# Block 0 of the convolution kernels: each group's doubling and products behind its own powers, and three modulation vectors computed in the convolution stage

## The chip, the cores and the metric

One core of one Trainium2 chip. Its engines run beside each other, each through its own instructions in a fixed order, and wait for each other by semaphores: TensorE (matmuls, and the loads of their stationary operand), VectorE, ScalarE (functions from tables, and copies), GpSimd, and the queues that start DMA transfers, of which SyncE's (SP) and GpSimd's are used here. The metric is the device time of one execution in microseconds; less is better. A kernel's time is the median of several runs.

## The reference

A sequence x of 2048 tokens by 576 channels passes two residual branches, each behind a layer norm that a conditioning vector c modulates. The first branch is a diagonal state space model, computed as a long convolution; the second a dense layer of width 4608 with relu:

```
mod = silu(c) @ w_mod                   # 6 vectors of 576: sa, ca, ga, sb, cb, gb
h = layernorm(x) * (1 + ca) + sa
dt = exp(log_dt);  A = -exp(log_A_real) + 1j*A_imag;  C = (C_real + 1j*C_imag) * dt
K[d, l] = 2 * Re( sum_n C[d, n] * exp(A[d, n] * dt[d] * l) )     # n < 128, l < 2048
x = x + ga * ( causal_convolution(h, K) + h * D_skip )           # by FFT in the reference
h = layernorm(x) * (1 + cb) + sb
x = x + gb * ( relu(h @ w1) @ w2 )
```

All of it is in 32-bit floating point.

## The kernel before, in words

The convolution kernels K are built first. Position l is split into a high and a low part, so that exp(A dt l) is a product of a factor W1 (16 high parts, with C in it) and a factor W2 (32 low parts), and K is a small matmul over the 128 states for each channel. The 576 channels go through in six groups of 96 (`first`), and the 2048 positions in four blocks of 512. `first` makes block 0; W1, W2 and the higher powers are also written to memory (`W1d`, `W2d`, `Zd`), from which `rest` builds the other blocks later.

For one group g:

- `turns`: six small pairs of matmuls give the phase in turns for 22 exponents; ScalarE rounds them to integers (k) and VectorE subtracts (L143). The matmuls go to three PSUM banks (tag "ph"), which the products' bank and the modulation's also come from.
- `exps`: ten pairs of matmuls in the same banks, and exp on ScalarE.
- `half_values`, once for the odd and once for the even low parts: sine and cosine on ScalarE, and products with the exponentials, the sines' on VectorE (L177, L178), the cosines' on GpSimd. With the odd half goes `start`, which writes the first column of W1 (L201, L202). There are two W1 buffers.
- `powers`: sines and cosines of four powers into a PSUM tile Z, of which there is one, times the exponentials (L216).
- `doubling`: W1 grows from 1 to 2, 4, 8 and 16 columns by complex products with Z on VectorE (L241 to L245); the adds of the last step are on GpSimd.
- `products`: 384 matmuls, each of 16 columns, in pairs for one channel (L255). `rows` copies the result for storing.

ScalarE's operations in this stage are kept in the order in which the program is written; on the other engines a scheduler sets the order, by its own estimates and by what depends on what, and from then on it is fixed. The scheduler sees the tiles: a tile from a pool of n buffers waits until the tile n places before it is no longer used. In the loop over g the program writes: odd values of g+1, rows of g-1, first half of the doubling of g, even values of g+1, second half of the doubling of g, powers of g+1, turns and exponentials of g+2, products of g.

The modulation vectors come from a generator (`mod`), which the group stage advances: silu(c) is spread over 128 columns (cb) and multiplied with a vector's part of w_mod, two halves of ten matmuls each. It makes ga, ca, sa, sb and cb in the group stage, their weights lying in the five W2 buffers. gb is made by `mod_gb` at the end of block 0's convolution. This convolution (`conv(0)`) loads x, normalizes it, transforms it and the kernel by matmuls and VectorE butterflies, multiplies, transforms back, adds, normalizes again (with cb and sb) and transposes the result for the dense layer. Its tiles lie where those of the group stage lay, so it starts when that stage has ended. Then `ffn` runs the dense layer for four blocks of 512 tokens (first matmul hps, L892, second acc, L917), with `rest` and the convolutions of the later blocks between its matmuls.

Of the kernel before, what the change touches and what calls it, by code (L numbers as in the profile page):

```python
# [10 lines left out]
F32 = mybir.dt.float32  # L11
# [7 lines left out]
P = 128  # L19
L = 2048  # L20
D = 576
# [18 lines left out]
class KGen:  # L40
# [19 lines left out]
    def setup(self, I):  # L60
        nc, pc, k = self.nc, self.pc, self.k
        v = nc.vector.tensor_tensor
        tmp = lambda n: self.pt.tile([G, NG, P], F32, tag="W1", bufs=2, name=n)
        lar, ai = tmp("lar"), tmp("ai")
# [67 lines left out]

    def turns(self, g):

        F = []
        for s0, n in ((0, 8), (17, 8), (32, 6)):
            k = self.pt.tile([P, 8, G], I32, tag="k", bufs=3, name=f"k_{g}")[:, :n]
            f = k.bitcast(F32)
            for a in (0, n // 2):
                b = a + n // 2  # L140
                ph = self.times(g, self.zz[0], s0 + a, n // 2)
                self.act(k[:, a:b], ph, AF.Copy)
                self.nc.vector.tensor_tensor(f[:, a:b], ph, k[:, a:b], op=ALU.subtract)  # L143
            F.append(f)
        return F

# [73 lines left out]
    def doubling(self, g):  # L220
# [4 lines left out]
        for i, m in enumerate((1, 2, 4, 8)):  # L225
# [5 lines left out]
            for u in (slice(0, 1), slice(1, 2)) if m > 2 else (slice(0, 2),):  # L231
# [13 lines left out]
                add(out[:, u, :, 1], t[:, :, :, 1], T[:, :, :, 0], op=ALU.add)  # L245
            if m == 2:
                yield

# [14 lines left out]
    def first(self, mod):  # L263

        nc, k = self.nc, self.k
        self.W1, self.Z, W2s, EF, ke = {}, {}, {}, {}, None

        def raw(g):
            if g < NG:
                F = self.turns(g)  # L270
                EF[g] = self.exps(g), F

        def odd(g):
            if g < NG:
                E, F = EF[g]
                W2s[g] = [
                    self.pt.tile([P, 2, 32, H], F32, tag="W2", bufs=5, name=f"W2_{2 * g + u}")
                    for u in range(2)
                ]
                self.half_values(g, W2s[g], E[2:4], F[0], True)  # L280

        def even(g):
            if g < NG:
                E, F = EF[g]
                self.half_values(g, W2s[g], E[0:2], F[1], False)
                for u in range(2):
                    nc.sync.dma_start(
                        out=k.W2d[2 * g + u], in_=W2s[g][u].rearrange("p r b c -> p (r b c)")
                    )

        def pw(g):
            if g < NG:
                E, F = EF.pop(g)
                self.powers(g, E[4], F[2])
                zs = self.Z[g][1]
                for u in range(2):
                    nc.sync.dma_start(out=k.Zd[2 * g + u], in_=zs[:, :, :, u * H : u * H + H])
# [12 lines left out]
        even(0)  # L310
        pw(0)
        next(mod)
        raw(1)
        ps = None
        for g in range(NG):
            odd(g + 1)
            if ps is not None:
                rows(g - 1, ps)
            step = self.doubling(g)
            next(step)  # L320
            next(mod, None)
            even(g + 1)
            next(step, None)
            for u in range(2):
                nc.sync.dma_start(
                    out=k.W1d[2 * g + u], in_=self.W1[g][:, u].rearrange("p a r c -> p (a r c)")
                )
            pw(g + 1)
            raw(g + 2)
            if g % 3 == 0:  # L330
                ke = self.pt.tile([P, 16, 72], F32, tag="ke", bufs=1, name=f"ke_{g}")
            ps = self.bank(f"kps_{g}")[:, :384].rearrange("p (q a) -> p q a", a=16)
            for u in range(2):
                self.products(ps, self.W1[g], W2s[g][u], u)
        rows(NG - 1, ps)

# [106 lines left out]
class Body:  # L443
# [41 lines left out]
    def mod(self, kg):  # L485
# [9 lines left out]
        for i, nm in names:  # L495
            w = ws[nm] = pt.tile([P, 5, D], F32, tag="W2", bufs=5, name=f"wm_{nm}")
            self.mod_weights(w, slice(i * D, (i + 1) * D))
# [6 lines left out]
        yield  # L504
        m = {}
        ga = kg.pc.tile([P, 2, PC], F32, name="m_ga")
        for i, nm in names:
            t = ga if nm == "ga" else self.cst.tile([P, 2, PC], F32, name=f"m_{nm}")
            for h in range(2):
                ps = kg.bank(f"mps_{nm}")[:, :PC]  # L510
                self.mod_product(ps, cb, ws[nm][:, :, h * PC : (h + 1) * PC])
                if nm == "ca":
# [3 lines left out]
                elif nm == "sa":  # L516
                    nc.vector.tensor_tensor(t[:, h], ps, ga[:, h], op=ALU.mult)
                elif nm == "cb":
                    nc.vector.tensor_scalar(t[:, h], ps, 1.0, None, op0=ALU.add)
                else:  # L520
                    nc.vector.tensor_copy(t[:, h], ps)
            m[nm] = t
            self.m = {k: v.rearrange("p h c -> p (h c)") for k, v in m.items() if k != "ga"}
            yield
# [15 lines left out]

    def mod_gb(self):

        cb = self.half("cb").rearrange("p a b -> p (a b)")[:, : 5 * P]
        cb = cb.rearrange("p (k c) -> p k c", c=P)
        self.mod_lhs(cb)
        t = self.m["gb"]
        for h in range(2):
            w = self.spec("wm_gb").rearrange("p a b c -> p (a b c)")[:, : 5 * PC]
            w = w.rearrange("p (k c) -> p k c", c=PC)
            self.mod_weights(w, slice(5 * D + h * PC, 5 * D + (h + 1) * PC))  # L550
            ps = self.cps.tile([P, 512], F32, tag="cps", name="mps_gb")[:, :PC]
            self.mod_product(ps, cb, w)
            self.nc.scalar.activation(t[:, h * PC : (h + 1) * PC], ps, AF.Copy)

    def main(self, ctx, kg):
        nc, tc = self.nc, self.tc
        self.sm = ctx.enter_context(tc.tile_pool(name="sm", bufs=1))
        self.m["gb"] = self.sm.tile([P, D], F32, name="m_gb")
        self.fcU, self.fcK, self.gc = (
# [535 lines left out]
```

## Time and profile before

| | us |
|---|---|
| median of 3 runs | 1543.28 (1539.92 to 1550.67) |
| the profiled execution | 1545.74, of it the span 1543.9 |
| TensorE matmuls busy in the span | 1311.2 (85%) |
| VectorE | 928.5 (60%) |
| ScalarE | 480.2 (31%) |
| GpSimd | 168.5 (11%) |

The stages in the span: setup and groups from 0 to 229, block 0's convolution to 329.7, then the dense layer. Busy shares over the whole span say little about the first two stages, in which every engine has idle time; the rows below are taken from these stages. A row's line number is that of the kernel before.

### The profile page before, as it was taken

What the parts mean: (1) busy time and instruction counts of PE and PEld (TensorE: products, weight loads), DVE (VectorE), ACT (ScalarE), POOL (GpSimd) and SP (SyncE); (2) the same over time, 40 slices, a digit from 0 to 9 for tenths busy, and PEclk for the clock granted to TensorE, in tenths of its full rate; (3) what the DMA queues carried; (4) which work ended last, traced back from release to release, by engine and by line L of the source; (5) the groups of instructions that cost most, each with busy time, mean ns of one, the idle gap of its engine ahead of it and who ended that gap; (6) DMA issues with size and microseconds to landing.
All of it is one profiled execution on the core that took longest, in us unless ns stands there. A gap on an engine that the chain in (4) does not pass through costs nothing.

```text
span 1543.9 us, 26164 instructions
## 1 busy us (share of the span) xinstructions
PE 1311.2 (85%) x10664; PEld 1036.8 (67%) x10664; DVE 928.5 (60%) x1396; ACT 480.2 (31%) x885; POOL 168.5 (11%) x271
## 2 busy tenths in 40 slices
PE   6665534379998899669899999999999999999997
PEld 4455433257787677447677777777787788888885
DVE  4645457979975558876684688936499831111112
ACT  4645414022222134014222432243432233233221
POOL 1433431000001010000101001000000000000000
PEclk9766656689999999779999999999999999999998
DMA  6533356346769758436986889667699656766662
GB/s 211 214 129 129 145 221 248 134 157 213 264 219 374 254 191 327 168 146 189 351 292 211 286 322 330 230 177 254 212 341 366 221 172 196 213 195 196 198 196 70
DMA packets 116903, 345.99 MB, mean 224 GB/s; under 512 B 19568, under 2 KB 21008, under 8 KB 105776
## 3 DMA queue, kind: packets, MB, share of 16 engines
q1 hardware_dynamic: 98432, 218.88, 43.4%
q0 software_dynamic: 18128, 124.86, 21.5%
q8 instruction: 83, 1.36, 0.4%
q10 hardware_dynamic: 224, 0.59, 0.1%
q14 instruction: 36, 0.29, 0.1%
HBM read 260.53 MB, written 83.76 MB: 223 GB/s over the span
## 4 chain that ended last, share of the span: by engine, by line
PE 51%; DVE 19%; issue 18%; DMA 9%; ACT 2%; POOL 1%; SPq 0%; POOLq 0%; ACTq 0%; DVEq 0%
PE hps L892 18%; PE acc L917 17%; PE kps L399 5%; PE ps_f L628 3%; PE ph L117 3%; DVE Y L759 2%; DVE T L757 2%; DMA w<-L1d 2%; DMA w<-L2d 2%; PE kps L255 2%; PE ps_i L766 1%; DMA Ud<-U 1%; DMA kt<-kd 1%; DVE T L242 1%; DMA L1d<-w 1%
## 5 line engine op out<-in xcount | busy, mean ns | idle before, releaser
L917 PE MATMUL acc<-hh,w 128*128 128x512 f32 x1296 | 429.7, 406 | 7.7 <-DMA w<-L2d 4.9
L892 PE MATMUL hps<-xh,w 128*128 128x512 f32 x1152 | 394.8, 403 | 0.0
L917 PE MATMUL acc<-hl,w 128*128 128x512 f32 x720 | 284.4, 408 | 20.9 <-DVE hl L898 20.8
L898 DVE SCALAR_TENSOR_TENSOR hl<-hps,hh 128x512 fp32r<-128x512 f32 x144 | 98.8, 686 | 323.8 <-ACT hh L897 323.6
L917 PEld LDWEIGHTS acc<-hh,w 128*128 128x128 f32 x1296 | 245.7, 191 | 63.6 <-DMA w<-L2d 6.2
L892 PEld LDWEIGHTS hps<-xh,w 128*128 128x128 f32 x1152 | 219.3, 192 | 47.5
L892 PE MATMUL hps<-xl,w 128*128 128x512 f32 x576 | 232.1, 403 | 0.0
L897 ACT ACTIVATE hh<-hps 128x512 fp32r<-128x512 f32 x144 | 86.1, 598 | 354.6 <-PE hps L892 351.9
L875 ACT ACTIVATE w<-r 128x576 fp32r<-128x576 f32 x144 | 98.8, 686 | 282.4 <-issue 188.0
L917 PEld LDWEIGHTS acc<-hl,w 128*128 128x128 f32 x720 | 137.7, 192 | 51.6 <-DVE hl L898 22.3
L892 PEld LDWEIGHTS hps<-xl,w 128*128 128x128 f32 x576 | 110.5, 192 | 23.7
L866 ACT ACTIVATE w<-r 128x640 fp32r<-128x640 f32 x144 | 105.3, 732 | 31.1 <-DMA L1d<-w 23.5
L892 PE MATMUL hps<-xs,w 128*128 128x512 f32 x288 | 101.3, 420 | 11.6 <-DMA w<-L1d 6.9
L399 PEld LDWEIGHTS kps<-W1r,W2r 128*32 128x32 f32 x3456 | 69.3, 146 | 37.8 <-issue 28.8
L399 PE MATMUL kps<-W1r,W2r 128*32 128x48 f32 (+2 forms) x3456 | 79.9, 238 | 12.6 <-issue 11.7
L759 DVE TENSOR_TENSOR Y<-Y,T 128x1152 f32<-128x1152 f32 x64 | 84.5, 1348 | 0.1
L629 ACT ACTIVATE Z<-ps_f 128x288 f32<-128x288 f32 x128 | 52.1, 409 | 78.7 <-PE ps_f L628 76.4
L117 PE MATMUL ph<-dl,zt 96*128 96x384 f32 (+1 forms) x72 | 22.9, 469 | 61.7 <-DVE k L143 50.8
L892 PEld LDWEIGHTS hps<-xs,w 128*128 128x128 f32 x288 | 54.2, 193 | 26.7 <-DMA w<-L1d 8.6
L766 PE MATMUL ps_i<-V,gc 128*128 128x288 f32 x128 | 43.9, 482 | 32.7 <-DVE V L642 14.8
L255 PE MATMUL kps<-W,W 128*32 128x16 f32 x2304 | 39.3, 216 | 36.1 <-issue 24.8
L628 PE MATMUL ps_f<-kt,fcK 128*128 128x288 f32 x128 | 46.2, 465 | 27.7 <-DVE kt L700 18.0
(177 smaller groups left out, 1515.7 us busy)
## 6 DMA issues: line engine op xcount, KB each, us to landing
r<-in_w_dram SPq DMA_DIRECT2D x144, 320.0 KB, 3.6
r<-in_w_dram SPq DMA_DIRECT2D x144, 288.0 KB, 3.3
w<-L1d SPq DMA_DIRECT2D x108, 320.0 KB, 3.0
w<-L2d SPq DMA_DIRECT2D x108, 288.0 KB, 3.2
W2r<-W2d POOLq DMA_DIRECT2D x18, 1536.0 KB, 8.7
W2d<-W SPq DMA_DIRECT2D x12, 1536.0 KB, 6.0
Ua<-Ud POOLq DMA_DIRECT2D x15, 1152.0 KB, 9.8
W<-W1d POOLq DMA_DIRECT2D x18, 768.0 KB, 10.0
```

What stands on the lines that cost most here:

```text
L117: self.nc.tensor.matmul(o, z[:, c, g], self.dl[:, s0 : s0 + n], start=(c == 0), stop=(c == 1))
L255: self.nc.tensor.matmul(ps[32 * dd : 32 * dd + 32, 12 * u + q, :], W2[:, r, :, ch], W1[:, u, :, r, ch], start=(r == 0), stop=(r == 1),)
L399: nc.tensor.matmul(ps[32 * dd : 32 * dd + 32, q, :], W2[:, r, :, ch], W1[:, :, r, ch], start=(r == 0), stop=(r == 1),)
L628: nc.tensor.matmul(o, fc[:, n2, c, :], src(n2), start=True, stop=True)
L759: v(y, y, T, op=op or ALU.add)
L766: nc.tensor.matmul(ps[:, :PC], self.gc[:, n2, c, :], V[:, n2, c], start=(c == 0), stop=(c == 1))
L866: nc.scalar.activation(w[:, 0], r, AF.Copy)
L875: nc.scalar.activation(w[:, 0:D], r, AF.Copy)
L892: nc.tensor.matmul(ps, a, x, start=(i == 0), stop=(i == 13))
L897: nc.scalar.activation(hh, ps, AF.Relu)
L898: nc.vector.scalar_tensor_tensor(hl, ps, 0.0, hh, op0=ALU.max, op1=ALU.subtract)
L917: nc.tensor.matmul(acc[i], a, x, start=(f == 0 and j in (0, 3, 6, 9, 12)), stop=(f == NF - 1 and j in (2, 5, 8, 11, 13)),)
```

## The change

`doubling` no longer stops halfway. `odd`, `even` and `pw` become one function, `values`, and the loop is written in another order: doubling of g, store of W1, products of g, values and powers of g+1, turns and exponentials of g+2. The row copies of g are called from within `turns`, behind the first of its three parts. Of the modulation vectors, only ga, ca and sa are made in the group stage; their weights and two setup tiles change places in the W1 and W2 buffers. sb, cb and gb are made in the convolution stage by `mod_late`, one half of a vector each sixth step from step 42 on, with ScalarE doing the copy out of PSUM.

```diff
-    def turns(self, g):
+    def turns(self, g, then):
...
             F.append(f)
+            if s0 == 0:
+                then()
...
                 add(out[:, u, :, 1], t[:, :, :, 1], T[:, :, :, 0], op=ALU.add)
-            if m == 2:
-                yield
...
+        def raw(g, then=lambda: None):
+            F = self.turns(g, then)
+            EF[g] = self.exps(g), F
+
+        def values(g):
+            E, F = EF.pop(g)
+            W2 = W2s[g] = [
+                self.pt.tile([P, 2, 32, H], F32, tag="W2", bufs=5, name=f"W2_{2 * g + u}")
+                for u in range(2)
+            ]
+            self.half_values(g, W2, E[2:4], F[0], True)
+            self.half_values(g, W2, E[0:2], F[1], False)
+            for u in range(2):
+                nc.sync.dma_start(out=k.W2d[2 * g + u], in_=W2[u].rearrange("p r b c -> p (r b c)"))
+            self.powers(g, E[4], F[2])
...
         raw(0)
         next(mod)
-        odd(0)
+        values(0)
+        raw(1)
         next(mod)
-        even(0)
-        pw(0)
-        next(mod)
-        raw(1)
-        ps = None
         for g in range(NG):
-            odd(g + 1)
-            if ps is not None:
-                rows(g - 1, ps)
-            step = self.doubling(g)
-            next(step)
-            next(mod, None)
-            even(g + 1)
-            next(step, None)
+            self.doubling(g)
             for u in range(2):
                 nc.sync.dma_start(
                     out=k.W1d[2 * g + u], in_=self.W1[g][:, u].rearrange("p a r c -> p (a r c)")
                 )
-            pw(g + 1)
-            raw(g + 2)
...
             for u in range(2):
                 self.products(ps, self.W1[g], W2s[g][u], u)
-        rows(NG - 1, ps)
+            if g == 0:
+                next(mod)
+            if g + 1 < NG:
+                values(g + 1)
+            if g + 2 < NG:
+                raw(g + 2, lambda: rows(g, ps))
+            else:
+                rows(g, ps)
...
-        names = ((2, "ga"), (1, "ca"), (0, "sa"), (3, "sb"), (4, "cb"))
+        names = ((2, "ga", "W1", 2), (1, "ca", "W1", 2), (0, "sa", "W2", 5))
...
-    def mod_gb(self):
+    def mod_late(self):
...
+        cb = self.cv.tile([P, 5, P], F32, tag="cb", name="cb")
         self.mod_lhs(cb)
...
+        for i, nm in ((3, "sb"), (4, "cb"), (5, "gb")):
+            t = self.m[nm]
+            for h in range(2):
+                w = self.cv.tile([P, 5, PC], F32, tag="wm", bufs=2, name=f"wm_{nm}")
+                self.mod_weights(w, slice(i * D + h * PC, i * D + (h + 1) * PC))
+                ps = self.cps.tile([P, 512], F32, tag="cps", name=f"mps_{nm}")[:, :PC]
+                self.mod_product(ps, cb, w)
+                self.nc.scalar.activation(
+                    t[:, h * PC : (h + 1) * PC], ps, AF.Copy, bias=1.0 if nm == "cb" else 0.0
+                )
+                yield
...
-            for _ in self.conv(0):
+            late = self.mod_late()
+            for i, _ in enumerate(self.conv(0)):
+                if i > 40 and i % 6 == 0:
+                    next(late, None)
+            for _ in late:
                 pass
-            self.mod_gb()
```

What this does to the fixed orders is seen at three places. A row is a line of the kernel in question, an operation and its tiles; a number behind a tile's name tells tiles of one name apart.

TensorE, around the products of group 0 (kps; ph are the matmuls of turns, with zt, and of exponentials, with zr). Before, behind the exponentials of group 2:

```order
L117 MATMUL ph_709<-dl,zr 128x384 x2
L117 MATMUL ph_714<-dl,zr 128x288 x2
L117 MATMUL ph_718<-dl,zr 128x288 x2
L255 MATMUL kps_723<-W_0_380,W_0_373 32x16 x96
L255 MATMUL kps_723<-W_0_380,W_1_374 32x16 x96
L539 MATMUL mps_cb<-wm_cb,cb 128x288 x10
```

Now, behind those of group 1, with the modulation's ca and sa on both sides:

```order
L117 MATMUL ph_492<-dl,zr 128x288 x2
L117 MATMUL ph_496<-dl,zr 128x288 x2
L518 MATMUL mps_ca<-wm_ca,cb 128x288 x10
L255 MATMUL kps_554<-W_0_374,W_0_367 32x16 x96
L255 MATMUL kps_554<-W_0_374,W_1_368 32x16 x96
L518 MATMUL mps_sa<-wm_sa,cb 128x288 x10
L117 MATMUL ph_818<-dl,zt 128x384 x2
```

In all groups the products moved ahead of the turns and exponentials of the group two further on.

VectorE, around the doubling of group 3 (W_3 is its W1; W_8, W_9 and W_4 are W2 and W1 of group 4; k are the turns). Before, the odd values and the start of group 4 stood inside the doubling of group 3, behind its first operation:

```order
L241 TENSOR_TENSOR t<-W_3_1303,Zp_1376 128x192
L143 TENSOR_TENSOR k_1401<-ph_1407,k_1401 128x384
L143 TENSOR_TENSOR k_1412<-ph_1413,k_1412 128x288
L143 TENSOR_TENSOR k_1412<-ph_1418,k_1412 128x288
L200 TENSOR_TENSOR Tc<-cc,s_1663 128x192
L177 TENSOR_TENSOR W_8_1661<-s_1663,E_1450 128x384
L178 SCALAR_TENSOR_TENSOR W_8_1661<-s_1663,E_1441 128x8x48
L177 TENSOR_TENSOR W_9_1662<-s_1663,E_1450 128x384
L178 SCALAR_TENSOR_TENSOR W_9_1662<-s_1663,E_1441 128x8x48
L201 TENSOR_TENSOR W_4_1668<-tc,Tc 128x2x48
L202 TENSOR_TENSOR W_4_1668<-tc,Tc 128x2x48
L242 TENSOR_TENSOR T<-W_3_1303,Zp_1376 128x192
```

Now the doubling of group 3 follows the powers of group 3 (L218) and the turns of group 5:

```order
L218 TENSOR_TENSOR Zp_1533<-Zp_1533,E_1252 128x384 x2
L143 TENSOR_TENSOR k_1547<-ph_1548,k_1547 128x384
L143 TENSOR_TENSOR k_1547<-ph_1553,k_1547 128x384
L243 TENSOR_TENSOR t<-W_3_1499,Zp_1533 128x192
L143 TENSOR_TENSOR k_1561<-ph_1562,k_1561 128x384
L143 TENSOR_TENSOR k_1561<-ph_1567,k_1561 128x384
L143 TENSOR_TENSOR k_1572<-ph_1573,k_1572 128x288
L143 TENSOR_TENSOR k_1572<-ph_1578,k_1572 128x288
L244 TENSOR_TENSOR T<-W_3_1499,Zp_1533 128x192
L246 TENSOR_TENSOR W_3_1499<-t,T 128x2x48
L247 TENSOR_TENSOR W_3_1499<-t,T 128x2x48
```

No operation of another group's W1 stands inside a doubling any more.

The SP queue at the end of the group stage (kd is the store of block 0's kernels, r are weights of the dense layer). Before:

```order
L340 DMA kd_1_58<-ke_1835 64x1152 x2
L850 DMA r_2978<-in_w_dram 128x640
L850 DMA r_2980<-in_w_dram 128x640
L854 DMA r_2982<-in_w_dram 128x576
L854 DMA r_2990<-in_w_dram 128x576
```

Now:

```order
L322 DMA kd_1_58<-ke_1666 64x1152 x2
L507 DMA wm_sb<-in_w_mod_dram 128x4x288
L510 DMA wm_sb<-in_w_mod_dram 64x288
L507 DMA wm_sb<-in_w_mod_dram 128x4x288
L510 DMA wm_sb<-in_w_mod_dram 64x288
L835 DMA r_2984<-in_w_dram 128x640
L835 DMA r_2986<-in_w_dram 128x640
L839 DMA r_2988<-in_w_dram 128x576
```

The weights of sb moved in between. In the dense layer the orders are as before, but for one VectorE operation of `rest` that now stands ahead of the first hl.

## Rows read from the trace of the kernel before

**Rows 1.** Stages: us; busy us and (instructions) of PE, PEld, DVE, ACT, POOL; clock, DMA, GB/s.
```profile
149.00:159.00 10.00, 7.45 (x388) 6.95 (x388) 2.62 (x7) 5.12 (x9) 4.94 (x8) 0.84 0.02 5
...
201.00:217.00 16.00, 7.22 (x432) 6.90 (x434) 11.62 (x24) 2.04 (x5) 10.06 (x13) 0.61 0.91 329
...
245.00:330.00 85.00, 43.61 (x137) 30.31 (x138) 77.59 (x144) 20.24 (x55) 4.61 (x8) 0.73 0.34 124
```

**Rows 2.** Timeline, one turn: start, us, engine, line, operation [idle before <-releaser].
```profile
137.71 0.49 ACT L49 ACTIVATE Zp<-k 128x384 f32<-128x384 f32 x1 [7.84 <-DVE T L242]
...
140.66 1.97 PE L117 MATMUL ph<-dl,zt 96*128 96x384 f32 x6 [11.98 <-DVE k L143]
...
141.71 1.37 ACT L49 ACTIVATE k<-ph 128x384 int32<-128x384 f32 x3 [1.24 <-PE ph L117]
142.23 1.34 DVE L143 TENSOR_TENSOR k<-ph,k 128x384 f32<-128x384 f32 x3 [0.43 <-ACT k L49]
...
149.39 3.47 PE L255 MATMUL kps<-W,W 128*32 128x16 f32 x215
...
151.22 0.82 ACT L49 ACTIVATE s<-k 128x768 f32<-128x768 f32 x1
...
153.74 0.54 DVE L178 SCALAR_TENSOR_TENSOR W<-s,E 128x384 f32<-128x384 f32 x1
...
157.57 0.93 PE L255 MATMUL kps<-W,W 128*32 128x16 f32 x41 [1.57 <-issue]
...
158.60 0.26 DVE L201 TENSOR_TENSOR W<-tc,Tc 128x96 f32<-128x96 f32 x1 [4.31 <-POOL W L183]
...
169.73 0.49 ACT L49 ACTIVATE Zp<-k 128x384 f32<-128x384 f32 x1 [7.84 <-DVE T L242]
```

**Rows 3.** Timeline, the tail: products of groups 4 and 5, doubling of group 5.
```profile
201.30 0.94 DVE L242 TENSOR_TENSOR T<-W,Zp 128x768 f32<-128x768 f32 x1
...
202.57 2.27 SPq L325 DMA_DIRECT2D W1d<-W  x2
202.60 2.92 PE L255 MATMUL kps<-W,W 128*32 128x16 f32 x179 [0.66 <-POOL W L245]
...
204.76 0.35 DVE L241 TENSOR_TENSOR t<-W,Zp 128x192 f32<-128x192 f32 x1
...
208.58 2.16 PE L255 MATMUL kps<-W,W 128*32 128x16 f32 x128 [3.07 <-issue]
...
213.23 0.94 DVE L242 TENSOR_TENSOR T<-W,Zp 128x768 f32<-128x768 f32 x1
...
215.15 2.14 PE L255 MATMUL kps<-W,W 128*32 128x16 f32 x127 [4.40 <-issue]
...
216.59 0.49 ACT L49 ACTIVATE ke<-kps 128x384 f32<-128x384 f32 x1 [12.67 <-PE kps L255]
...
229.03 0.49 ACT L49 ACTIVATE ke<-kps 128x384 f32<-128x384 f32 x1 [11.95 <-PE kps L255]
```

**Rows 4.** Timeline, group 0: modulation product ga, and ScalarE's values.
```profile
25.15 5.70 PE L539 MATMUL mps_ga<-wm_ga,cb 128*128 128x288 f32 x20
...
27.01 0.81 ACT L49 ACTIVATE s<-k 128x768 f32<-128x768 f32 x1
...
37.58 0.81 ACT L49 ACTIVATE s<-k 128x768 f32<-128x768 f32 x1 [7.29 <-DVE W L178]
...
40.39 0.56 ACT L49 ACTIVATE Zp<-c,halfpi 128x384 f32<-128x384 f32 x1
```

**Rows 5.** Timeline, from the convolution to the dense layer.
```profile
322.21 7.02 PE L539 MATMUL mps_gb<-wm_gb,cb 128*128 128x288 f32 x20
...
323.59 0.29 DVE L829 TENSOR_TENSOR xs<-ps_t,xs 64x128 fp32r<-64x128 f32 x1
...
329.74 0.73 PE L892 MATMUL hps<-xs,w 128*128 128x512 f32 x2 [0.50 <-ACT m_gb L553]
```

**Rows 6.** DMA issues: tensors, queue, count, KB each, median us to landing.
```profile
wm_gb<-in_w_mod_dram SPq DMA_DIRECT2D x2, 576.0 KB, 5.5
```

More of the change, by code (lines that the diff above doesn't have):

```diff
@@ L62, in setup @@
         v = nc.vector.tensor_tensor
-        tmp = lambda n: self.pt.tile([G, NG, P], F32, tag="W1", bufs=2, name=n)
+        tmp = lambda n: self.pt.tile([G, NG, P], F32, tag="W2", bufs=5, name=n)
         lar, ai = tmp("lar"), tmp("ai")
@@ L266, in first @@
         self.W1, self.Z, W2s, EF, ke = {}, {}, {}, {}, None
[L268 to L297, printed above, removed]
+        def raw(g, then=lambda: None):
[12 more added lines that the diff above has]
+            self.powers(g, E[4], F[2])
+            zs = self.Z[g][1]
+            for u in range(2):
+                nc.sync.dma_start(out=k.Zd[2 * g + u], in_=zs[:, :, :, u * H : u * H + H])
         def rows(g, ps):
@@ L492, in mod @@
         nc.sync.dma_start(out=ct[0:64, 4:5], in_=I["c"][512:576].unsqueeze(1))
-        names = ((2, "ga"), (1, "ca"), (0, "sa"), (3, "sb"), (4, "cb"))
+        names = ((2, "ga", "W1", 2), (1, "ca", "W1", 2), (0, "sa", "W2", 5))
         ws = {}
-        for i, nm in names:
-            w = ws[nm] = pt.tile([P, 5, D], F32, tag="W2", bufs=5, name=f"wm_{nm}")
+        for i, nm, tag, bufs in names:
+            w = ws[nm] = pt.tile([P, 5, D], F32, tag=tag, bufs=bufs, name=f"wm_{nm}")
             self.mod_weights(w, slice(i * D, (i + 1) * D))
@@ L504, in mod @@
         yield
-        m = {}
+        self.m = {}
         ga = kg.pc.tile([P, 2, PC], F32, name="m_ga")
-        for i, nm in names:
+        for i, nm, _, _ in names:
             t = ga if nm == "ga" else self.cst.tile([P, 2, PC], F32, name=f"m_{nm}")
@@ L511, in mod @@
                 self.mod_product(ps, cb, ws[nm][:, :, h * PC : (h + 1) * PC])
-                if nm == "ca":
+                if nm == "ga":
+                    nc.vector.tensor_copy(t[:, h], ps)
+                elif nm == "ca":
                     nc.vector.scalar_tensor_tensor(
@@ L515, in mod @@
                     )
-                elif nm == "sa":
+                else:
                     nc.vector.tensor_tensor(t[:, h], ps, ga[:, h], op=ALU.mult)
[L518 to L523, printed above, removed]
+            self.m[nm] = t.rearrange("p h c -> p (h c)")
             yield
@@ L539, in mod_product @@
             self.nc.tensor.matmul(ps, cb[:kp, k, :], w[:kp, k], start=(k == 0), stop=(k == 4))
-    def mod_gb(self):
-        cb = self.half("cb").rearrange("p a b -> p (a b)")[:, : 5 * P]
-        cb = cb.rearrange("p (k c) -> p k c", c=P)
+    def mod_late(self):
+        cb = self.cv.tile([P, 5, P], F32, tag="cb", name="cb")
         self.mod_lhs(cb)
[L546 to L553, printed above, removed]
+        for i, nm in ((3, "sb"), (4, "cb"), (5, "gb")):
[9 more added lines that the diff above has]
+                yield
     def main(self, ctx, kg):
@@ L557, in main @@
         self.sm = ctx.enter_context(tc.tile_pool(name="sm", bufs=1))
-        self.m["gb"] = self.sm.tile([P, D], F32, name="m_gb")
+        for n in ("sb", "cb", "gb"):
+            self.m[n] = self.sm.tile([P, D], F32, name=f"m_{n}")
         self.fcU, self.fcK, self.gc = (
```

## The prediction, written before the changed kernel was run

> **What bounds the kernel now.** The change touches the first 330 us of the span: the group stage (0 to 229 us) and block 0's convolution (to 329.7 us). What follows, the dense layer with the later convolutions between its matmuls, keeps its order on every engine but for one swap on VectorE, so the question is how much earlier it starts. I read the table of stages first (how busy the engines are in one stage), then the timeline of one turn of the group loop from release to release, then the stage's tail, where the same work stands with less beside it.
>
> No engine is full in the group stage: in the 10 us in which one group's products run, TensorE is busy 7.5 us, ScalarE 5.1 and VectorE 2.6 [rows 1]. It is a ring of waits. In the turn shown [rows 2], the doubling of group 2 ends on VectorE at 137.7. The powers of group 3 on ScalarE had waited for that, since both use the single Z bank. Then the six argument steps ("turns") of group 4 run, the last three from 140.66 to 143.57, 0.97 us each; then its exponentials. The products of group 2, whose W1 was ready some 10 us ago, stand behind these in TensorE's order and start at 149.39, 6.3 us after the last turn on ScalarE (143.08). They run to 158.5 with pauses. Only then can VectorE write W1 of group 4 (L201, at 158.60: there are two W1 buffers), and the doubling of group 3 stands behind L201 in VectorE's order. From the Z bank's release at 137.71 to the next at 169.73 that is 32 us a group.
>
> **The products' price.** They are 384 matmuls and as many weight loads. 128 of them take 2.16 us when nothing holds them, so 384 take 6.5 [rows 3]. The stream is cut after each 128 of them, and there TensorE waits for "issue", nothing that the profile shows: 1.57 us in the turn shown, with the DMA engines 2% busy [rows 1, 2], but 3.07 and 4.40 us in the tail, with them 91% busy and W1d's store issued at 202.57 [rows 1, 3]. So one group's products cost 9.2 us (149.39 to 158.60) in a quiet window and 14.0 us (202.60 to 216.59) in a busy one; the last group's took 12.4 (to 229.03). I take the pauses for the fetching of the instructions themselves, which goes by DMA; that is a reading of where they stand, not a row.
>
> **What the change does to the ring.** Group g's doubling now stands behind its own powers and the turns of the next group, its products directly behind that, and the values of the next group behind the products. In TensorE's order products(g) come ahead of the turns and exponentials of group g+2; before, they came behind them. In VectorE's order the doubling is one piece, with no L201 of the next group in it. Let D be the end of a doubling on VectorE and K the end of its products.
> From K to the next D: the turns of the next-but-one group had to wait for K on TensorE, except one that is already made; five at 0.97 us are 4.8 [rows 2]. Then the rest of the doubling: undisturbed it takes 9.41 us, 204.76 to 214.17 [rows 3], of which 0.35 is already done among the turns: 9.05.
> From D to K: the first products start 0.36 us after the last VectorE operation (202.24 to 202.60) [rows 3], then the products.
> So a turn is 4.8 + 9.05 + 0.36 + products = 14.2 + products.
> The exponentials leave this chain: on ScalarE they take from the last turn to the next sine 151.22 - 143.08 = 8.1 us [rows 2], beside a doubling of 9.05. So does the next group's values work, beside the products: four sine products end 3.1 us after the sine starts [rows 2], the even half and the powers take 3.4 us (37.58 to 40.95) [rows 4], and with the Z product of 0.6 us that is about 7.4 us after D. Products of 9.2 cover it; if they were under 7, it would be the chain.
>
> **Where the products lie between the bounds.** W1d's stores (two of 768 KB a group) are issued right after the doubling and now run beside the products, as in the tail; W2d's follow later. I take one pause as in the tail (3.07 in place of 1.57) and the others quiet: 10.7 us for groups 0 to 3, and 12.4 for group 5, beside the constants' loads as in the tail. Bounds are 9.2 and 14.0 for all.
>
> **The sum of the group stage.** Group 0's sine starts at 27.0 as before [rows 4]. Odd half 3.1, even half and powers 3.4, and some 0.4 for the copy of ga between: turns from 34.0, done at 38.8. Exponentials: TensorE is free 6.3 us after the last turn on ScalarE, at 44.7. mps_ca follows (5.70, as the row of ga [rows 4]): 50.4. Products 10.7: K(0) = 61.1. mps_sa now stands between K(0) and the turns: 5.7, then six turns 5.8, 9.05, 0.36 and 10.7: K(1) = 92.7. Two turns of the ring at 24.9 each: K(3) = 142.5. Group 4 has D at 156.4. Group 5 has no turns left behind it: 7.4 and 9.4 us after that D is 173.2, and 0.36 + 12.4 gives K(5) = 186.0, where it was 229.0 [rows 3]: **43 us less**. With 9.2 everywhere it is 52 less, with 14.0 everywhere 28: every microsecond on the products counts five times.
>
> **The convolution.** mps_gb stood ahead of the dense layer: hps began at 329.74, while VectorE had split the last of the transposes at 323.88 [rows 5]; 5.9 us go. mps_gb took 7.02 us where the same matmuls took 5.70 for ga [rows 4, 5]: behind the transposes its first part ran slower. The first hps will stand in that place, and I charge it the 1.3. Six halves of w_mod are read and multiplied inside the convolution, where VectorE is busy 77.6 of 85 us and TensorE 43.6 [rows 1]: sb's and cb's matmuls are hidden as long as no transform comes late. What can: (a) sb's 1.33 MB are queued on SP ahead of the dense layer's first weights, whose splitting stands on VectorE and ScalarE ahead of the first normalization. At the 329 GB/s of rows 1 that is 4.0 us; the x load and kt's run meanwhile, so between 0 and 4.0, I take 2. (b) gb's second half can load only when cb's second half has freed its buffer, lands 5.5 us later [rows 6], and its matmuls stand ahead of the inverse transform on TensorE. Between 0 and one landing, I take 2. The copy of cb (one VectorE operation) moves to a place where VectorE waits for x: nothing, as long as it does. Net -5.9 + 1.3 + 2 + 2 = **-0.6** (-4.6 to +4.9).
>
> Together 44 us. The profiled execution took 1545.74 us for a span of 1543.9, so 1502; it lies 2.5 us above the median of the three runs, 1543.28, from which I predict **1499 us**.
>
> **Rivals.** A kernel of this size can be told from no change at about 1%, 15 us.
> 1. *The fetch pauses as in the tail's worst* (14.0 us each): for it, W1d's store beside the products; against, only 1.5 MB are in flight then, where the tail had the constants and Zd too. 52.4 - 5 x 4.8 + 0.6 = 29 us less, 1514.
> 2. *The pauses go away*, because TensorE now waits ahead of each product group and its instructions are there in time: products 6.5, the values chain of 7.4 binds, a turn is 21.3, K(5) = 165: 1479. Against: in the tail TensorE had waited for GpSimd before 202.60 and the pauses came all the same [rows 3]. The Trainium skill ("Runtime: NRT & Kernel Launch", section "Instruction fetch mechanics") says that the next block of 256 instructions is fetched by DMA while the present one executes and that this is mostly hidden. By that rule this rival holds; the trace, with pauses of 1.57 to 4.40 us, does not agree.
> 3. *The gain is eaten*: three pauses of 4.4 us in each group make 19.7 us of products, and 52.4 - 5 x 10.5 leaves nothing: 1543.
> 4. *Slower*: the stores W1d, W2d and Zd, 4.9 MB a group, fall into a shorter turn, and so into the fetch. This decides from 19.8 us of products on; for 1% slower they need 22.9, pauses of 5.5. At 6 us a pause the products take 24.5, five of them cost 76.5 against the 52.4, and the time is 1567. No row has a pause over 4.40.
>
> **Chances and range.** Forecast (products of 9.2 to 13) 0.70, at 1484 to 1508; rival 1 (13 to 16 us) 0.14, 1508 to 1523; rival 2 0.08; rival 3 0.05; rival 4 0.03. The range 1484 to 1516 takes the forecast and the nearer half of rival 1, and some of rival 2's edge. Faster by over 1% are the first three cases, 0.92; within 1% 0.05; slower 0.03.
>
> **What the changed profile should show.** Products of group 0 start near 50 us and those of group 5 end near 186; two ends of products about 25 us apart; the turns of a group released by TensorE (products) and not by the Z bank; 10 to 11 us from the first to the last of a group's products, with "issue" pauses; hps directly behind the transposes, about 44 us earlier than 329.7. The prediction is wrong if the products stay below 8 us or above 14, if the turns start well after K, if the convolution waits over 4 us for the first weights, or if the dense layer, starting earlier, does not end earlier by as much.

## The result, and the profile after

The changed kernel took **1496.14 us** in the median of four runs (1495.45 to 1500.85); the kernel before, beside it, 1541.6 (1537.13 to 1550.67). The ratio is 0.9704, with a 95% interval of 0.9655 to 0.9754: **45.5 us less**, where 44 were forecast. Of the profiled execution (1500.85) the span is 1499.0. Line numbers are now those of the changed kernel.

The stages, in the columns of [rows 1]: the products of group 4, those of group 5, and the convolution from its first normalization to the first hps.

```profile
161.70:173.20 11.50, 7.10 (x384) 6.57 (x384) 8.52 (x22) 6.18 (x10) 10.57 (x14) 0.60 0.40 157
...
179.50:193.40 13.90, 6.79 (x384) 6.37 (x384) 0.58 (x1) 0.04 (x1) 2.85 (x3) 0.62 0.77 275
213.70:289.50 75.80, 46.18 (x169) 31.06 (x169) 74.62 (x132) 19.54 (x53) 5.67 (x10) 0.85 0.47 168
```

A group's products now take VectorE, ScalarE and GpSimd along: in group 4's window VectorE is busy 8.5 of 11.5 us, where it was 2.6 of 10. The next rows are one turn, from the end of group 2's doubling to that of group 3's, and answer to [rows 2] (timeline: start, us, engine, line, operation, idle before and its releaser).

```profile
107.61 0.94 DVE L244 TENSOR_TENSOR T<-W,Zp 128x768 f32<-128x768 f32 x1
...
108.02 0.29 PE L255 MATMUL kps<-W,W 128*32 128x16 f32 x2 [1.82 <-POOL W L246]
...
108.98 2.52 PE L255 MATMUL kps<-W,W 128*32 128x16 f32 x153 [0.30 <-POOL W L247]
...
113.12 1.01 POOL L246 TENSOR_TENSOR W<-T,T 128x384 f32<-128x384 f32 x1
...
113.54 0.94 PE L255 MATMUL kps<-W,W 128*32 128x16 f32 x39 [2.05 <-issue]
...
115.15 1.60 PE L255 MATMUL kps<-W,W 128*32 128x16 f32 x89 [0.67 <-POOL W L247]
...
117.85 1.87 PE L255 MATMUL kps<-W,W 128*32 128x16 f32 x101 [1.10 <-issue]
119.65 1.33 PE L117 MATMUL ph<-dl,zt 96*128 96x384 f32 x3
120.38 1.13 ACT L49 ACTIVATE k<-ph 128x384 int32<-128x384 f32 x2 [3.47 <-PE ph L117]
120.90 1.20 DVE L143 TENSOR_TENSOR k<-ph,k 128x384 f32<-128x384 f32 x2 [3.17 <-ACT k L49]
...
134.01 0.94 DVE L244 TENSOR_TENSOR T<-W,Zp 128x768 f32<-128x768 f32 x1
134.41 0.30 PE L255 MATMUL kps<-W,W 128*32 128x16 f32 x2 [2.61 <-ACT s L49]
```

The ring is the forecast one: the turns (L117) stand directly behind the products, ScalarE waits for them (3.47 us) and VectorE for what ScalarE rounds (3.17), and one round of the ring takes 26.4 us (108.02 to 134.41) where it took 32. But the products took 11.7 us, not 10.7: beside two pauses under "issue" there is a wait for GpSimd (0.67 us here, 2.0 in groups 3 and 4). The additions that complete the second half of W1 (L246, at 113.12) stood in GpSimd's order behind a product for W1 of the next group and two of its W2.

The tail, which answers to [rows 3], with group 5's W1 store in flight:

```profile
179.14 0.94 DVE L244 TENSOR_TENSOR T<-W,Zp 128x768 f32<-128x768 f32 x1
...
180.41 2.29 SPq L302 DMA_DIRECT2D W1d<-W  x2
180.44 3.41 PE L255 MATMUL kps<-W,W 128*32 128x16 f32 x212 [0.66 <-POOL W L247]
...
187.29 2.17 PE L255 MATMUL kps<-W,W 128*32 128x16 f32 x128 [3.44 <-issue]
192.38 0.93 PE L255 MATMUL kps<-W,W 128*32 128x16 f32 x42 [2.93 <-issue]
193.36 0.49 ACT L49 ACTIVATE ke<-kps 128x384 f32<-128x384 f32 x1 [19.63 <-PE kps L255]
```

Group 5's products end at 193.4, where they ended at 229.0; 186.0 was forecast. Then from the convolution to the dense layer, which answers to [rows 5]:

```profile
247.35 5.67 PE L518 MATMUL mps_gb<-wm_gb,cb 128*128 128x288 f32 x20 [2.29 <-DMA wm_gb<-in_w_mod_dram]
252.95 4.15 PE L751 MATMUL ps_i<-V,gc 128*128 128x288 f32 x16
...
256.21 0.44 DVE L634 TENSOR_TENSOR K<-W 128x288 f32<-128x288 f32 x1
256.58 0.80 DVE L757 TENSOR_TENSOR x<-ps_i,x 128x288 f32<-128x288 f32 x2
...
289.46 1.22 PE L877 MATMUL hps<-xs,w 128*128 128x512 f32 x2 [1.53 <-DVE xs L814]
```

The dense layer starts behind the transposes' last VectorE operation, at 289.5 instead of 329.7. gb's product waits for its weights and stands ahead of the inverse transform (ps_i), but VectorE, which uses ps_i (L757), comes to it without idling.

How steady these places are, three traces of this same kernel show (the second and third are the runs named a1_again and e7_w1_late below):

| trace of the changed kernel | 1 | 2 | 3 | forecast | before |
|---|---|---|---|---|---|
| mps_sa, us | 10.0 | 5.7 | 7.1 | 5.7 | |
| group 5's products end | 193.4 | 188.6 | 190.3 | 186.0 | 229.0 |
| from there to the first hps | 96.1 | 97.4 | 96.8 | 100.1 | 100.7 |
| first hps starts | 289.5 | 285.9 | 287.1 | 286.1 | 329.7 |
| from there to the end of the span | 1209.5 | 1214.5 | 1212.1 | 1214.2 | 1214.2 |

So 40.2 to 43.8 us are gained ahead of the dense layer, and the layer itself varies by 5 us from trace to trace of one kernel. The 4.6 us that it is shorter in the first trace are within that.

### The profile page after: what moved, and what is told of

It reads as the page before. It is cut to its first block, busy times and chain, and to the rows that moved or that the text cites. A ratio compares the mean times of both kernels' runs of the same rounds, so it can differ in the third digit from the quotient of the medians.

```text
span 1499.0 us, 26182 instructions
## 1 busy us (share of the span) xinstructions
PE 1314.2 (88%) x10664; PEld 1037.4 (69%) x10664; DVE 928.2 (62%) x1392; ACT 481.4 (32%) x889; POOL 168.7 (11%) x271
## 4 chain that ended last, share of the span: by engine, by line
PE 43%; DVE 23%; issue 19%; DMA 9%; ACT 3%; POOL 1%; SPq 0%; POOLq 0%; ACTq 0%; DVEq 0%
PE acc L902 15%; PE hps L877 14%; PE kps L381 4%; DVE T L742 4%; DVE Y L744 4%; PE ps_f L613 3%; PE ph L117 3%; DMA Ud<-U 2%; PE kps L255 2%; DMA L1d<-w 1%; PE ps_i L751 1%; DMA kt<-kd 1%; DMA Ua<-Ud 1%; DVE T L350 1%; DVE Y L738 1%
## 5 line engine op out<-in xcount | busy, mean ns | idle before, releaser
L851 ACT ACTIVATE w<-r 128x640 fp32r<-128x640 f32 x144 | 105.4, 732 | 24.4 <-DMA L1d<-w 20.5
L255 PEld LDWEIGHTS kps<-W,W 128*32 128x32 f32 x2304 | 39.2, 151 | 47.3 <-issue 22.2
L1000 POOL DMA_DIRECT2D out_dram<-x x16 | 8.7, 546 | 511.9 <-DVE x L998 511.9
L613 PE MATMUL ps_f<-kt,fcK 128*128 128x288 f32 x128 | 45.0, 450 | 21.2 <-DMA wm_sb<-in_w_mod_dram 15.5
## 6 DMA issues: line engine op xcount, KB each, us to landing
Ua<-Ud POOLq DMA_DIRECT2D x15, 1152.0 KB, 10.5
```

The source lines that it names most:

```text
L255: self.nc.tensor.matmul(ps[32 * dd : 32 * dd + 32, 12 * u + q, :], W2[:, r, :, ch], W1[:, u, :, r, ch], start=(r == 0), stop=(r == 1),)
L613: nc.tensor.matmul(o, fc[:, n2, c, :], src(n2), start=True, stop=True)
L851: nc.scalar.activation(w[:, 0], r, AF.Copy)
```

## The experiments

Times of before are those beside the same runs. "End" is where group 5's products end.

**The two parts alone.** One kernel has the new loop, but sb and cb in the group stage and gb ahead of the dense layer; the other has the old loop with the three vectors in the convolution.

```diff
# e1_loop_only, from the changed kernel
-        names = ((2, "ga", "W1", 2), (1, "ca", "W1", 2), (0, "sa", "W2", 5))
+        names = (
+            (2, "ga", "W1", 2), (1, "ca", "W1", 2), (0, "sa", "W2", 5), (3, "sb", "W2", 5), (4, "cb", "W2", 5),
+        )
-            if g == 0:
+            for _ in range((2, 1, 0, 0, 0, 0)[g]):
                 next(mod)
# e2_mod_only, from the kernel before
-        names = ((2, "ga"), (1, "ca"), (0, "sa"), (3, "sb"), (4, "cb"))
+        names = ((2, "ga"), (1, "ca"), (0, "sa"))
...
-            self.mod_gb()
+                if i > 40 and i % 6 == 0:
+                    next(late, None)
```

> The new order of block 0's groups alone; the vectors sb and cb stay in the group stage (behind the products of groups 0 and 1), gb stays ahead of the dense layer. Theory (the order of the groups carries most of the gain): sb and cb each add a product like that of sa, 5.7 to 10 us, to the ring, so that the products of group 5 end 11 to 20 us later than the 193.4 of the changed kernel, at 204 to 213; from there to the first hps it takes 100.7 us as before the change and not 96.1; together 1496 + 11 to 20 + 4.6 = 1512 to 1521. Rival A (sb and cb are hidden in the ring): group 5 ends at 193 to 196 and the time is 1501. Rival B (the moved vectors carry most of the gain): 1530 or more.

> The moved vectors alone, with the old order of block 0's groups. Theory: what goes is two products in the group stage (5.7 and 7.2 us by their rows, at most 13 together, and only as far as the ring waited for them) and 4.6 us between the last group and the first hps; 1541.6 minus 5 to 18 = 1524 to 1537. Rival B (the moved vectors carry most of the gain): 1512 or less.

The loop alone: 1516.72 us against 1544.91, ratio 0.9816 (0.9772 to 0.986); end 198.1, first hps at 300.6. The vectors alone: 1534.87, ratio 0.9936 (0.9914 to 0.9957); end 221.6, first hps at 318.3. Both times are as expected, the end of the first is earlier (198.1, not 204 to 213). Behind sa (8.15 us) and sb (5.70) only 9.3 us passed until group 1's products began; in the changed kernel 12.4 pass behind sa alone, so some 3 us of sb were covered. The loop is worth 28 us, the vectors 10: the loop carries most of the gain, as the theory of the first had it. The two sum to 38, and both together gave 42 to 45; the intervals leave open whether that difference is real.

**The changed kernel again, and sa ahead of the products.**

```diff
# e5_sa_first: sa's step of the generator moves ahead of the loop
         next(mod)
+        next(mod)
         for g in range(NG):
...
-            if g == 0:
-                next(mod)
```

> The changed kernel again, beside the three next runs, which are to be compared with it. Theory (what the product of sa cost, 10.0 us and not 5.7, is the granted clock behind group 0's products, 0.50 there, and not the order of the work): in this trace of the same kernel it may lie anywhere between 5.7 and 11.4 us, with the clock beside it. Rival (the order of the work makes it): 10 us again, within 0.5. Time 1494 to 1501.

> The changed kernel with the product of sa ahead of group 0's products (behind that of ca) and not behind them. Theory: there it has the full clock and takes 5.7 us, group 0's products start 5 to 5.7 us later and end 4.5 to 5.5 us later, and the turns of group 2 start at about 65 instead of 69.5: group 5 ends 4 us earlier, 1492; if the clock grants 5.7 us behind the products as well, it is worth nothing. Rival (whichever comes second pays the low clock): the products of group 0 take 3 to 5 us longer and group 5 ends at 192 to 194.

The repeat: 1502.33 us against 1544.56, ratio 0.9705 (0.9678 to 0.9731). Its mps_sa took 5.70 us. The columns are those of [rows 1]; the first two rows are group 0's products and mps_sa of the repeat:

```profile
51.30:60.38 9.08, 6.59 (x385) 6.26 (x384) 4.76 (x12) 3.78 (x7) 9.08 (x13) 1.00 0.39 153
60.38:66.08 5.70, 5.70 (x24) 3.53 (x21) 2.38 (x6) 0.00 (x0) 1.50 (x3) 1.00 1.01 410
```

and the same stretches of the first trace, mps_sa in two parts:

```profile
49.92:59.47 9.55, 6.64 (x386) 6.30 (x385) 4.76 (x12) 3.77 (x7) 9.55 (x14) 0.93 0.40 160
59.47:64.00 4.53, 4.53 (x12) 2.92 (x10) 0.00 (x0) 0.00 (x0) 0.92 (x2) 0.50 0.97 389
64.00:69.44 5.44, 5.44 (x12) 2.92 (x12) 2.38 (x6) 0.00 (x0) 0.00 (x0) 0.59 0.54 185
```

Instructions and their order are the same. The granted clock during mps_sa was 1.00 in the one, 0.50 and 0.59 in the other (of full speed, 2.4 GHz; 0.50 is the level of 1.2). So the 10.0 us are a matter of the clock, and not of where sa stands; behind the same products it was granted either way.

With sa first the time was 1503.27, ratio 0.9729 (0.971 to 0.9749), no better, and the end came at 197.1, later than in any trace of the changed kernel. mps_sa had its 5.70 us, but group 0's products, pushed behind it, took 12.9 us. The reason is in their last rows:

```profile
61.20 2.15 PE L255 MATMUL kps<-W,W 128*32 128x16 f32 x128 [1.03 <-issue]
68.77 0.70 PE L255 MATMUL kps<-W,W 128*32 128x16 f32 x31 [5.41 <-issue]
```

and in the window of this pause:

```profile
61.00:69.50 8.50, 2.89 (x160) 2.75 (x160) 0.64 (x2) 0.00 (x0) 0.91 (x2) 0.83 0.86 326
```

A pause of 5.41 us, longer than any in the kernel before, with the DMA engines 86% busy: the W2 stores of group 1 are issued at 59.0 here and in the repeat, and fell beside mps_sa in the repeat, beside the products here. Theory and rival both missed: the clock was not what decided. But this explains only part of the late end. Of the 8.5 us by which it is later than in the repeat (197.1 against 188.6), 3.5 are there when group 4's products end (173.3 against 169.8); another 3.6 lie in group 5's products, which took 17.4 us instead of 13.8, with pauses of 4.09, 4.24 and 1.29, though the DMA engines moved as much beside them (3.8 MB). Why they were longer is open.

**The pauses and the stores.** One kernel leaves out the stores of groups 1 to 5; two others move those of W1.

```diff
# e3_no_stores (the same for Zd and W1d; rest() loads k.W2d[h % 2])
-            for u in range(2):
+            for u in range(2 if g == 0 else 0):
                 nc.sync.dma_start(out=k.W2d[2 * g + u], in_=W2[u].rearrange("p r b c -> p (r b c)"))
# e7_w1_late, e13_w1_moved: keep(g) stores W1d of g
             if g + 1 < NG:
                 values(g + 1)
+                keep(g)
# e13_w1_moved alone: these stores stay in the order of the program
+                self.tc.keep_in_program_order(nc.sync.dma_start(
```

> The changed kernel without the stores of W2, W1 and Z of groups 1 to 5; the later blocks load those of group 0 in their place, so their rows are other numbers. Theory (TensorE's pauses in a group's products are its instructions being fetched, and the stores beside them make them longer): the pauses under issue in groups 1 to 5, 1.7 to 3.4 us each in the changed kernel, fall to 0.4 to 2 us, the products of group 5 from 13.8 to 10 to 11 us, and all of group 5's end comes 4 to 8 us earlier; 1496 - 4 to 8 = 1488 to 1492. Rival (the pauses have nothing to do with the traffic): they keep 1.7 to 3.4 us, group 5 ends within 2 us of 193.4, 1494 to 1498.

> The changed kernel with the stores of a group's W1 issued behind the next group's W2 and Z stores, so that they run beside the turns and not beside the products (that of group 5 stays). Theory (traffic beside the products makes the pauses for instructions longer): the pauses of groups 1 to 4 fall from 1.7 to 2.9 us to 0.9 to 1.3, as without any stores; group 5 ends 3 to 5 us earlier, 1491 to 1493. Rival A (the stores now reach into the next products, which start 14 us later): pauses as before, no change. Rival B (the stores delay those of W2, whose buffers come free later): group 5 ends later by 1 to 3 us.

> The changed kernel with the stores of W1 of groups 0 to 4 held back on SyncE, in a fixed order, until the next group's W2 and Z stores are issued, so that they run beside the turns and not beside the products. (In the run named e7_w1_late the same edit without the fixed order left every engine's order of instructions as it was; it measured the changed kernel a third time.) Theory (traffic beside the products makes the pauses for instructions longer): issue pauses of groups 1 to 4 fall from 1.1 to 3.1 us to 0.9 to 1.3, as without any stores; group 5 ends at 183 to 187 instead of 188.6 to 193.4. Rival A (only their number counts): pauses as before. Rival B (the W1 stores now reach into the next products): the pauses fall in the first half of the products alone and the end moves by less than 2 us. The time moves by no more than the end of group 5 does, 0 to 7 us.

Without stores: 1493.32 us, ratio 0.9663 (0.9616 to 0.971), end 182.9. Group 5's products took 9.9 us instead of 13.8:

```profile
173.91 3.38 PE L255 MATMUL kps<-W,W 128*32 128x16 f32 x212 [0.65 <-POOL W L247]
178.25 2.08 PE L255 MATMUL kps<-W,W 128*32 128x16 f32 x128 [0.97 <-issue]
181.98 0.89 PE L255 MATMUL kps<-W,W 128*32 128x16 f32 x42 [1.65 <-issue]
```

All eight pauses of groups 1 to 5 are 0.87 to 1.65 us; in the changed kernel's trace they are 1.10 to 3.44. The theory holds for the pauses; the end came 5.7 to 10.5 us earlier than in the three traces of the changed kernel. The total does not show it: the interval of the ratio overlaps that of the changed kernel.

The first attempt at moving the stores (e7) moved nothing: the scheduler put them where they had been, and every engine's order came out as in the changed kernel. It is the third trace of the table (1499.33 us, ratio 0.9699, 0.9676 to 0.9722). With the order fixed (e13) the pauses of groups 1 to 4 fell to 0.73 to 1.38, as without stores, and the end came at 185.4. But the stores held back from groups 4 and 5 then met in the tail, where beside group 5's products four of them were issued instead of two, and the DMA engines moved 5.70 MB instead of 3.83:

```profile
170.83 3.41 PE L255 MATMUL kps<-W,W 128*32 128x16 f32 x212 [0.66 <-POOL W L247]
177.95 2.08 PE L255 MATMUL kps<-W,W 128*32 128x16 f32 x128 [3.71 <-issue]
184.42 0.94 PE L255 MATMUL kps<-W,W 128*32 128x16 f32 x42 [4.38 <-issue]
```

Group 5's products took 15.5 us, and from the end to the first hps it took 99.1 us instead of 96 to 97. The time was 1498.44 against 1545.21, ratio 0.9695 (0.9669 to 0.9722): not to be told from the changed kernel.

**GpSimd's additions.** In the last doubling, the second half's go to VectorE.

```diff
-                add = p if m == 8 else v
+                add = p if m == 8 and u.start == 0 else v
```

> The changed kernel with the last doubling's two additions of the second half on VectorE and not on GpSimd. Theory (the second half of the products waits for GpSimd, whose additions stand behind four multiplications of the next group): the waits for L246 and L247 inside the products, 0.7 us in group 2 and 2.0 us in groups 3 and 4, go, and VectorE has the 1.1 us to spare; group 5 ends 3 to 5 us earlier, 1491 to 1493. Rival (the pause for instructions only comes later in the same products): group 5 ends within 1 us of 193.4 and the time is the same.

The end came at 187.0, against 188.6 to 193.4. The waits for the second half's L246 and L247 inside the products are gone (in groups 4 and 5 the 0.66 us for the first half's L247 stays); of group 3's products these rows remain:

```profile
127.54 0.30 PE L255 MATMUL kps<-W,W 128*32 128x16 f32 x2 [1.72 <-POOL W L246]
128.50 3.94 PE L255 MATMUL kps<-W,W 128*32 128x16 f32 x249
135.37 2.16 PE L255 MATMUL kps<-W,W 128*32 128x16 f32 x128 [2.93 <-issue]
138.83 0.42 PE L255 MATMUL kps<-W,W 128*32 128x16 f32 x5 [1.29 <-issue]
```

In the changed kernel this group had a wait of 2.0 us for GpSimd and one pause of 2.86; now it has two pauses, 4.2 together, and takes 11.7 us instead of 12.6. The wait had covered a pause. And from the start of group 4's products to that of group 5's it took 19.2 us, 17.8 in the changed kernel, so that part of what the products gained was lost there. The time was 1498.71, ratio 0.9719 (0.9669 to 0.9769): no difference, as the rival had it, though not for its reason alone.

**Half the products**, to see how far they carry the ring.

```diff
-                for r in range(2):
+                for r in range(1):
...
-                        start=(r == 0),
-                        stop=(r == 1),
+                        start=True,
+                        stop=True,
```

> The changed kernel with half of block 0's products: per channel only the real parts are multiplied (192 matmuls a group and not 384), so its rows are other numbers. It measures how far the products carry the turn. In the repeated trace of the changed kernel ScalarE and VectorE stand idle for 3.4 us (113.0 to 116.5, 113.8 to 117.0) until group 2's products end. Theory (the products stand in the turn, with those 3.4 us in hand, behind which ScalarE's and VectorE's own work decides): each of the turns behind groups 1 to 4 gets 3 to 5 us shorter and not 6, group 0's and group 5's products 4 to 7 us; group 5 ends at 162 to 174 against 188.6 to 193.4; the time is 1470 to 1482. Rival A (the products alone set the turn): 5 x 6 + 7 us earlier, 153 or before. Rival B (they are hidden beside the other engines): only group 5's own 7 us, 182 or after. The pauses go on coming behind each 128 matmuls: one or two in a group.

1481.45 us against 1544.28, ratio 0.9576 (0.9544 to 0.9609); end 165.1. Groups 2, 3 and 4 start their products 21.7 us apart:

```profile
95.63 1.59 PE L255 MATMUL kps<-W,W 128*32 128x16 f32 x96 [1.77 <-POOL W L246]
101.82 1.59 PE L255 MATMUL kps<-W,W 128*32 128x16 f32 x96 [3.66 <-POOL W L246]
117.36 1.62 PE L255 MATMUL kps<-W,W 128*32 128x16 f32 x96 [1.77 <-POOL W L246]
123.56 1.63 PE L255 MATMUL kps<-W,W 128*32 128x16 f32 x96 [3.63 <-POOL W L246]
139.10 1.63 PE L255 MATMUL kps<-W,W 128*32 128x16 f32 x96 [2.05 <-POOL W L246]
```

A round of the ring lost 4.1 to 5.6 us (from 25.8 to 27.3 in the first two traces), not 6: the products stand in the ring, and what is behind them takes over. On ScalarE the next turns now follow its powers without a wait:

```profile
104.12 0.44 ACT L49 ACTIVATE zs<-c,halfpi 128x192 f32<-128x192 f32 x1
104.47 0.83 ACT L49 ACTIVATE k<-ph 128x384 int32<-128x384 f32 x2
```

That is the values chain, as expected, but it is not alone. The products of groups 2 to 4 still took 7.6 to 7.8 us, 3.6 to 4.4 of them the wait for GpSimd (L246), and those of group 2 ended at 103.4, about 1 us before ScalarE's powers (104.56). The run does not tell what the chain holds from what GpSimd holds. The expected pauses are missing in groups 1 to 4, since the waits for GpSimd lie over them; one of 3.71 us stands in group 5.

**A better version?** Two combinations: e8 is e4, e5 and e7 together (so e4 and e5, as e7 moved nothing), e14 is e4 and e13.

> All three edits together: the second half's additions on VectorE, the product of sa first, the stores of W1 late. Theory: the gains of the three add up, since they take away different waits: group 5 ends 8 to 12 us before the 193.4 of the changed kernel, and the first hps starts as much earlier; 1484 to 1489. Rival (given back in the dense layer, as the first trace with the additions moved may hint: 6.6 us earlier at the first hps, no difference in the median): 1494 to 1499.

> The same with the last doubling's second additions on VectorE as well: the two edits that a version better than the changed kernel would be made of. Theory: both waits inside the products go (GpSimd's, and the longer part of the pauses), products of groups 1 to 4 at 9.5 to 10.5 us instead of 11.4 to 12.8, group 5 ends at 179 to 184, first hps at 276 to 281, the time 5 to 9 us under the changed kernel's, ratio to before 0.964 to 0.967 against its 0.970. Rival (given back behind it, as in the run of all three edits): ratio 0.969 to 0.973.

e8: 1501.84 us against 1544.56, ratio 0.9723 (0.9701 to 0.9746), end 190.8; sa ahead of the products spoils it as in e5 (a pause of 4.33). e14: 1496.31 against 1545.21, ratio 0.9698 (0.9665 to 0.9732). Its products of groups 1 to 4 took 9.7 to 10.4 us, as expected, but group 5's 16.6, so that the end came at 185.6 and the first hps at 283.4, and the dense layer took 1213.5. Neither is shown to beat the changed kernel.

## Why the prediction was right, step by step

- **The ring** held in every trace of the new loop: products, turns, rest of the doubling, products. Its fixed part was forecast at 14.2 us from the end of a group's products to the start of the next; measured in the changed kernel are 13.5 to 14.7 (119.7 to 134.4 in the turn shown).
- **The products** were sized too small: 10.7 us forecast for groups 0 to 3, measured 9.6, 12.5, 11.7, 12.6, and 11.5 for group 4. The forecast took one pause of each group as long as in the tail and the other quiet, 3.07 and 0.98 us; measured they are 0.4 to 2.9 each, 2.5, 4.6, 3.2, 2.9 and 1.7 together in groups 0 to 4, so that only group 1 is over the charge. An argument step (ph) stands among the products of groups 1 to 3, 0.4 to 1.0 us. And in groups 2 to 4 there is a term that the forecast lacks, GpSimd: it charged 0.36 us for the first additions and overlooked that the second half's stand behind the next group's products of L201, L184 and L185. e14, with that wait and the longer pauses taken away, has 9.7 to 10.4. For group 5 the 12.4 became 13.8.
- **The fetch as cause of the pauses** was a reading. e3, e13 and e5 make the tie to DMA traffic a result: 0.87 to 1.65 us without stores, up to 5.41 beside W2's. That instructions are what is fetched is seen in the DMA rows of the same traces. In the window of group 5's products there is

```profile
q8 instruction: 2, 0.03, 0.9%
```

  two packets of some 16 KB on an instruction queue, and two pauses, behind 128 matmuls and as many loads each. Narrow windows tell when such a packet moves. In e5's pause of 5.41 us (63.36 to 68.77) the DMA rows from 63.40 to 66.20 have only the first of these queues; from 66.20 to 66.80 the second is there as well:

```profile
q1 hardware_dynamic: 111, 1.17, 103.2%
q8 instruction: 1, 0.02, 9.2%
```

  The packet moved only in the middle of the pause, 2.8 us and more after its begin, in which the DMA engines moved other packets, and TensorE went on 2.2 to 2.3 us later. In the quiet turn of [rows 2] the packet moved at 154.9, ahead of the pause (156.0 to 157.57), which ended 2.7 us behind it. All 137 pauses under "issue" inside the products, in the thirteen traces of before, the changed kernel and the experiments, end 2.0 to 3.2 us behind one such packet; in those under 2.0 us it moved before the pause began, in those over 2.5 us after it began. So the pause is the longer, the later the packet moves. Why TensorE needs 2 to 3 us behind the packet no run shows.

  Rival 2's rule (the Trainium skill, "Runtime: NRT & Kernel Launch", section "Instruction fetch mechanics") is that the next block is fetched while this one runs, and that this is mostly hidden. The first half agrees with the trace where the queues are quiet (the packet at 154.9); the second does not hold for this stream, not even there. What the rival said beyond it comes near: with the products short enough, e12's round is 21.7 us, where 21.3 were worked out from the values chain, though there the wait for GpSimd is as close.
- **mps_sa** at 5.7 us, taken from ga's row [rows 4], is right where the clock is granted in full and 4.3 short where it is not. The stretch behind it, from there to group 1's products, was sized too dear: 15.2 us (six turns, the rest of the doubling, the first additions), measured 12.4 to 12.5 in the three traces; VectorE does the first step of the doubling by the end of mps_sa (from 64.9 to 66.8 in the repeat), of which the forecast had only 0.35 us out of the way. In the first trace this hides 2.7 of the 4.3.
- Together the group stage gave 36 to 40 us and not 43.
- **The convolution** was forecast too dear: -0.6, measured -3.3 to -4.6. gb's halves landed in 5.7 us (5.5 in [rows 6]), but the second one ahead of ps_i cost nothing instead of 2, since VectorE was still at work. From the last products to the first normalization (L653) it took 20.4 us (193.36 to 213.72) against 18.9 (229.03 to 247.92), 1.5 for the 2 charged to sb's loads; it is 20.5 with the vectors moved alone and 19.7 with the loop alone. The first hps started slowly, as charged. The columns are those of [rows 1], from the first matmuls with xs to the next with xs, now and before:

```profile
289.46:294.73 5.27, 5.27 (x14) 4.21 (x15) 1.08 (x1) 0.00 (x0) 1.95 (x4) 0.59 0.98 344
329.74:333.06 3.32, 3.32 (x14) 2.73 (x15) 0.00 (x0) 0.00 (x0) 3.17 (x6) 1.00 0.59 181
```

  That is 1.95 us for the 1.3 charged, with a granted clock of 0.59 instead of 1.00.
- **The sum** came out since the two errors, 3 to 7 us in the group stage and 3 to 4 the other way in the convolution, nearly cancel. That is luck: nothing in the working ties one to the other. The first hps, forecast at 286.1, came at 285.9 to 289.5. In the first trace it came only 40.2 us earlier than before, and the rest of that execution's gain is the dense layer's 4.6, which is within its spread.
- **Rivals 3 and 4** did not come, but their mechanism is in e5: group 0's products took 3.3 us longer than in the first trace because other stores fell beside them.

## What to carry to other kernels

In a ring of waits, price every instruction that stands in it on every engine, the small ones on the slow engine too: behind a wait that is taken away, look for the next one that it covered. A transfer's place counts as much as its size; a store moved away from one stage's fetches falls beside another's. And when a stage's gain is under the spread of what follows (here 5 us), the trace of the stage can show it, the total can't.

## What the runs showed of the hardware

- Behind 128 of these matmuls and their loads (2.16 us of work) TensorE paused 0.7 to 1.7 us where the stores were away (groups 1 to 5 of e3, 1 to 4 of e13), and up to 5.41 us with the DMA engines 86% busy (e5).
- Each of the 137 pauses in thirteen traces ended 2.0 to 3.2 us behind a packet of some 16 KB on the instruction queue; the long ones are those whose packet moved late.
- The same product behind the same instructions took 5.70, 7.14 and 10.04 us in three traces of one kernel, by the granted clock (1.00; 0.79 in the second; 0.50 and 0.59).
